# First tiles and weights of a conformer block over two DMA queues, normalized on VectorE and multiplied tile by tile, with the last chunk's halo columns copied one block ahead

## Chip, cores, metric

One core of one Trainium2 chip runs the whole program. The metric is the device time of one execution in microseconds (us); lower is better. Quoted times are medians of several runs with the lowest and highest in brackets; a trace is of one execution only.

## The reference

One conformer block with batch 2, 4000 tokens, width D = 512 and F = 2048, in bf16. `_layernorm` has no weights. Cut to what matters:

```python
h = _layernorm(x)                                  # x: [2, 4000, 512]
x1 = x + 0.5 * (_silu(h @ w_ff1_a) @ w_ff1_b)      # w_ff1_a: [512, 2048]
h = _layernorm(x1)                                 # one attention head of width 512
q, k, v = h @ w_q, h @ w_k, h @ w_v
x2 = x1 + (softmax(q k^T * D**-0.5) v) @ w_o
h = _layernorm(x2) @ w_pw1                         # w_pw1: [512, 1024]
h = h[..., :D] * sigmoid(h[..., D:])
dc = sum over i of hp[:, i:i+T] * dw[i]            # depthwise, width 3, hp padded by 1 on each side
dc = (dc - mean) / sqrt(var + 1e-5)                # mean, var per channel over all tokens
x3 = x2 + _silu(dc) @ w_pw2
x4 = x3 + 0.5 * (_silu(_layernorm(x3) @ w_ff2_a) @ w_ff2_b)
return _layernorm(x4)
```

Two places count here. At the start nothing can be multiplied before the first rows of `x` are loaded, normalized and transposed, and before the first columns of `w_ff1_a` have come. And the batch norm needs the statistics of all tokens, so that everything after the depthwise convolution of the last chunk waits for it.

## The kernel before

The tokens go in chunks of 508 (four tiles of 127 rows); the last chunk has 444. While the first rows come in, PE is kept busy with matmuls on zeros (`warm`), so that its clock is up when the real ones begin (in the traces a 508-column matmul takes 0.42 us at the slow clock of the start and 0.216 in the regular flow). Each tile's rows are loaded in two parts (112 and 15 rows). Engines are written as DVE (VectorE), ACT (ScalarE), POOL (GpSimd), PE (TensorE) and SP (the queue that issues most DMAs). Cuts are marked with `# ...`.

The loads. Six of the eight parts of the first four tiles are issued by SP, then all weights:

```python
    def load_rows(self, dst, src, writes, eng):
        k = self.S.dsems[self.nxt("ld", 16)]
        return self.S.dma(eng, k, *[lambda e, lo=lo, hi=hi: e.dma_start(dst[lo:hi], src[lo:hi])
                                     for lo, hi in self.ROWS], writes=writes)

    # ... in program():
        for ti in range(TPC):                       # TPC = 4
            self.load_rows(self.XT[ti], self.x_flat[ti * TILE:(ti + 1) * TILE, :], [self.bx[ti]], "ACT" if ti == 1 else "SP")
        for k in range(self.NWA):                   # NWA = 8 pieces of w_ff1_a, 256 columns each
            self.load_wa(i["w_ff1_a"], k, "SP")
            self.load_wb(i["w_ff1_b"], 2 * k, 2 * k + 2)
            # ...
```

The first layer norm: statistics on DVE, the power -1/2 on POOL (`ln_factor`), the normalization of three tiles on ACT and of the last on DVE. A block is one tile (or a pair of tiles) times the first four 128-column groups of `w_ff1_a`; groups 0 and 1 lie in weight piece 0, groups 2 and 3 in piece 1.

```python
    def ln_tiles(self, c, sl, prepare=None, engs=("ACT", "ACT", "ACT", "DVE"), src=None, lag=2):
        # ... finish(ti): sign product on DVE if the engine is ACT, then ln_norm on engs[ti]
        for ti in range(TPC):
            # ...
            self.ln_stats(c, sl, ti, src)
            # ...
            if ti >= lag:
                finish(ti - lag)
                yield ti - lag
            if lag == 1 or ti == TPC - 1:
                self.ln_mean(sl, ti)
                self.ln_factor(sl, ti)
        for ti in range(TPC - lag, TPC):
            finish(ti)
            yield ti

    def head(self):

        self.warm(14)
        self.rings["ln"] = 1
        self.early = [self.sbank() for _ in range(4)]

        def blocks(lo, hi):
            for f, (ps, b_ps) in enumerate(self.early):
                out = ps[:, lo * TILE:hi * TILE].rearrange("p (t k) -> p t k", t=hi - lo)
                for cc in range(DC):
                    self.mm(out, self.Wa[:, cc, f * 128:(f + 1) * 128], self.lnT[0][:, lo:hi, cc, 0:TILE],
                            cc == 0, cc == DC - 1, [self.b_Wa[f * self.NWA // FC]] + self.b_lnT[0][lo:hi], b_ps)

        for ti in self.ln_tiles(0, 0, lag=1):
            if ti:
                self.transpose_pe(ti - 1, 0, "ACT", (self.Yb[ti - 1], self.b_Y[ti - 1]))
            if ti == 2:
                blocks(0, 1)
        blocks(1, 2)
        self.transpose_pe(TPC - 1, 0, "DVE", (self.Yb[TPC - 1], self.b_Y[TPC - 1]))
        blocks(2, 4)
```

The last chunk's convolution. `conv_a` forms the gated values `G` of one 128-channel block; `halo_left` writes, on POOL, the one column left of them (copied from the chunk before) and the zero column right of the sequence's end. `finish` runs the depthwise convolution of the preceding block, its statistics, and with `conv_scale` a power on POOL of 0.55 us.

```python
    def conv_a(self, t, jj):
        # ...
        elif t == NCK - 1:
            self.halo_left(t, jj)
            self.S.op("DVE", lambda e: e.scalar_tensor_tensor(
                out=out, in0=ps[:, 0:W], scalar=2.0, in1=th, op0=ALU.mult, op1=ALU.mult),
                reads=[b_ps, self.b_th[k]], writes=wr)
        # ...

    # ... the loop over the four blocks of the last chunk:
        for jj in range(DC):
            self.conv_b(last, jj)
            # ...
            self.conv_a(last, jj)
            if jj > 1:
                self.conv_shift(jj - 2)
            if jj:
                finish(jj - 1)
            else:
                # ...
```

The gate names `Gl` and `Gr`, the columns that the halo writes, among what it writes (`wr`), so it stands behind `halo_left` wherever that comes in the program.

Of the kernel before, what the change touches and what calls it, by code (L numbers as in the profile page):

```python
# [15 lines left out]
TILE = 127  # L16
TPC = 4
# [10 lines left out]
DC = D // 128  # L28
FC = F // 128
# [51 lines left out]
class Sync:  # L81
# [103 lines left out]
        return None  # L185

    def dma(self, e, dkey, *fns, reads=(), writes=()):
        req = self._required(reads, writes)
        prev = self.count[dkey]
        if prev > 0:  # L190
            v = req.get(dkey)
            if v is None or v.val < prev:
                req[dkey] = Ev(dkey, prev, {})
        self._emit_waits(e, req)
        for fn in fns:
            fn(self.eng[e]).then_inc(self.sem[dkey], 16)
            self.count[dkey] += 16
        ev = Ev(dkey, self.count[dkey], dict(self.clock[e]))
        self._bind(ev, reads, writes)
        return ev  # L200

# [45 lines left out]
class Conformer:  # L247
# [315 lines left out]
        k = self.S.dsems[16 + self.nxt("tr", 12)]  # L563
        return self.S.dma("SP", k, lambda e: e.dma_start_transpose(dst, src), reads=reads, writes=writes)

    def load_rows(self, dst, src, writes, eng):
        k = self.S.dsems[self.nxt("ld", 16)]
        return self.S.dma(eng, k, *[lambda e, lo=lo, hi=hi: e.dma_start(dst[lo:hi], src[lo:hi])  # L568
                                     for lo, hi in self.ROWS], writes=writes)

    def store(self, dst, src, reads, writes):
        k = self.S.dsems[36 + self.nxt("st", 8)]
# [126 lines left out]

    def head(self):  # L700

        self.warm(14)
        self.rings["ln"] = 1
        self.early = [self.sbank() for _ in range(4)]

        def blocks(lo, hi):
            for f, (ps, b_ps) in enumerate(self.early):
                out = ps[:, lo * TILE:hi * TILE].rearrange("p (t k) -> p t k", t=hi - lo)
                for cc in range(DC):
                    self.mm(out, self.Wa[:, cc, f * 128:(f + 1) * 128], self.lnT[0][:, lo:hi, cc, 0:TILE],  # L710
                            cc == 0, cc == DC - 1, [self.b_Wa[f * self.NWA // FC]] + self.b_lnT[0][lo:hi], b_ps)

        for ti in self.ln_tiles(0, 0, lag=1):
            if ti:
                self.transpose_pe(ti - 1, 0, "ACT", (self.Yb[ti - 1], self.b_Y[ti - 1]))
            if ti == 2:
                blocks(0, 1)
        blocks(1, 2)
        self.transpose_pe(TPC - 1, 0, "DVE", (self.Yb[TPC - 1], self.b_Y[TPC - 1]))
        blocks(2, 4)  # L720

    def ln_mean(self, sl, ti):
        self.S.op("DVE", lambda e: e.bn_aggr(self.mv[sl][:, ti, :], self.st[sl][:, ti, :]),
# [355 lines left out]
    def conv_a(self, t, jj):  # L1079

        ps, b_ps = self.pw1(t, jj)
        k, gs, W = jj % 2, t % 2, width(t)
        th = self.th[k][:, 0:W]
        out = self.G[gs][:, jj, 1:1 + W]
        wr = [self.b_G[gs][jj], self.b_Gl[gs][jj], self.b_Gr[gs][jj]]
        if t == NCK - 2 and jj >= self.KEEP:

            asb, b_asb = self.asb[jj % 3], self.b_asb[jj % 3]
            self.act(asb, ps[:, 0:CHUNK], AF.Copy, [b_ps], [b_asb], scale=2.0)

            def gate(eng):
                self.S.op(eng, lambda e: e.tensor_tensor(out=out, in0=asb, in1=th, op=ALU.mult),
                          reads=[b_asb, self.b_th[k]], writes=wr)
                self.halo_left(t, jj)
                self.halo_right(t, jj)

            return gate
        elif t == NCK - 1:
            self.halo_left(t, jj)
            self.S.op("DVE", lambda e: e.scalar_tensor_tensor(  # L1100
                out=out, in0=ps[:, 0:W], scalar=2.0, in1=th, op0=ALU.mult, op1=ALU.mult),
                reads=[b_ps, self.b_th[k]], writes=wr)
        else:
            self.S.op("DVE", lambda e: e.scalar_tensor_tensor(  # L1104
                out=out, in0=th, scalar=1.0, in1=ps[:, 0:W], op0=ALU.add, op1=ALU.mult),
                reads=[b_ps, self.b_th[k]], writes=wr)
        if t < NCK - 1:
            self.halo_left(t, jj)
        self.halo_right(t, jj)
# [230 lines left out]
    def program(self, any_score):  # L1340
        i = self.i
# [4 lines left out]
        self.scr = self.OT.rearrange("p c k -> p (c k)")[:, 0:512]  # L1346

        for ti in range(TPC):
            self.load_rows(self.XT[ti], self.x_flat[ti * TILE:(ti + 1) * TILE, :], [self.bx[ti]], "ACT" if ti == 1 else "SP")
        for k in range(self.NWA):  # L1350
            self.load_wa(i["w_ff1_a"], k, "SP")
            self.load_wb(i["w_ff1_b"], 2 * k, 2 * k + 2)
            if k == 3:
                self.load_x(1)
# [71 lines left out]
        last = NCK - 1  # L1426
# [53 lines left out]
        def copy_away():  # L1480
            while copies:
                copies.pop(0)()

        for jj in range(DC):
            self.conv_b(last, jj)
            if jj == DC - 1:
                self.act(self.nr1, self.onef, AF.Silu, [self.b_onef], [self.b_nr1])
            copy_away()
            self.conv_a(last, jj)
            if jj > 1:  # L1490
                self.conv_shift(jj - 2)
            if jj:
                finish(jj - 1)
            else:
                f, copy = self.depthwise(tail - 1, DC - 1)
                f()
                copies.append(copy)
# [129 lines left out]
```

## Time and profile before

| | before |
|---|---|
| time, median of 4 runs | 2045.07 us (2044.95 to 2045.14) |
| span of the profiled execution | 2040.1 us |
| PE busy | 2029.2 us |
| start of PE's regular flow of 508-column matmuls | 13.06 us after the span's start |
| last swish of the first chunk (end of the batch norm's wait) | starts at 1543.50 us |

The page and the timelines that matter are shown in the prediction below, where they are read. One more view: the chain that ended last, followed back through the first 16 us. Columns are start, duration and what; "issue" is time in which an engine waited for nothing that the profile shows.

```profile
4.44 4.27 DMA wff<-in_w_ff_a_dram
...
8.75 0.62 PE s L506 x8
...
10.75 0.44 DVE work L553
...
11.33 2.77 PE s L506 x20
```

Before these lines the chain runs along SP's queue, which issues row after row and then weights; it goes into the second piece of `w_ff1_a` (issued at 4.44, landed 4.27 us later), and from there through PE and a copy on DVE to the flow. The start of the flow: the last row of the head mixes its last short matmuls with the first four long ones, and the row of four after it begins one group (0.87 us) after the flow did. The trace of this kernel is of an execution that took 2043.90 us, faster than each of the four timed ones.

### The profile page before, as it was taken

How to read it: one execution, taken by the hardware profiler on the slowest of the kernel's cores; microseconds unless marked ns; L12 is line 12 of the kernel's file. 1: busy time of each engine (PE TensorE's matmuls, PEld its weight loads, DVE VectorE, ACT ScalarE, POOL GpSimd, SP SyncE). 2: the span in 40 equal slices, each digit the busy share in tenths (PEclk: the TensorE clock that was granted, in tenths of full speed). 3: DMA queues.
4: the chain of work that ended last, by engine and by line, in shares of the span. 5: the costliest groups of instructions: out<-in, count | busy, mean ns of one | idle time of the engine just before them, and what ended most of it. 6: DMA issues, size and time to landing. Idle time of an engine off the chain costs nothing.

```text
span 2040.1 us, 24550 instructions
## 1 busy us (share of the span) xinstructions
PE 2029.2 (99%) x9665; PEld 1029.8 (50%) x9667; DVE 1081.1 (53%) x2187; ACT 746.9 (37%) x1280; POOL 107.7 (5%) x235
## 2 busy tenths in 40 slices
PE   9999999999999999999999999999999999999998
PEld 5555555554444444445444444444455555555555
DVE  4234443334556667666766676667674444434433
ACT  3433333333333333333333333333345443443433
POOL 1000000000000000000000000000011000000000
PEclk9999999999999999999999999999999999999999
DMA  8222245320101111114421111111143111111111
GB/s 185 52 62 62 53 100 126 96 70 8 27 16 26 25 33 26 25 25 95 108 57 23 26 28 33 24 26 26 44 135 93 32 31 42 32 31 42 28 35 38
DMA packets 253122, 104.43 MB, mean 51 GB/s; under 512 B 193412, under 2 KB 252487, under 8 KB 252999
## 3 DMA queue, kind: packets, MB, share of 16 engines
q1 hardware_dynamic: 252751, 102.61, 20.9%
q8 instruction: 78, 1.28, 0.3%
q14 instruction: 45, 0.37, 0.1%
q10 hardware_dynamic: 248, 0.18, 0.0%
HBM read 33.77 MB, written 23.34 MB: 28 GB/s over the span
## 4 chain that ended last, share of the span: by engine, by line
PE 98%; DVE 1%; ACT 0%; DMA 0%; SPq 0%; POOL 0%; issue 0%; DVEq 0%; ACTq 0%
PE s L506 56%; PE y L506 42%; ACT work L556 0%; DVE wff L1206 0%; DMA wff<-in_w_ff_a_dram 0%; SPq L568 0%; POOL work L1215 0%; DVE work L553 0%; DVE wff L1100 0%; PE y L534 0%; ACT keys L556 0%; DVE work L1213 0%; SPq L560 0%; DVE work L869 0%; DVE work L952 0%
## 5 line engine op out<-in xcount | busy, mean ns | idle before, releaser
L556 ACT ACTIVATE work<-s 128x508 bf16<-128x508 f32 (+3 forms) x1060 | 622.7, 588 | 1211.8 <-PE s L506 1208.2
L506 PE MATMUL s<-work,wff 128*128 128x508 bf16 (+5 forms) x2624 | 628.3, 371 | 1.5 <-DVE work L553 0.8
L506 PE MATMUL s<-work,keys 128*128 128x508 bf16 (+1 forms) x2048 | 516.7, 374 | 0.1
L506 PE MATMUL y<-work,keys 128*128 128x508 bf16 (+2 forms) x2048 | 504.2, 373 | 0.4 <-DVE work L553 0.4
L506 PE MATMUL y<-wff,work 128*127 128x512 bf16 (+1 forms) x2000 | 501.4, 378 | 0.0
L952 DVE TENSOR_TENSOR work<-work 128x508 f32<-128x508 f32 (+2 forms) x496 | 334.6, 675 | 282.9 <-ACT work L556 281.8
L506 PEld LDWEIGHTS s<-work,wff 128*128 128x128 bf16 x2624 | 252.3, 98 | 278.0 <-issue 5.0
L506 PEld LDWEIGHTS y<-wff,work 128*127 128x127 bf16 x2000 | 274.4, 137 | 170.8
L506 PEld LDWEIGHTS s<-work,keys 128*128 128x128 bf16 x2048 | 199.4, 98 | 231.9 <-issue 0.6
L506 PEld LDWEIGHTS y<-work,keys 128*128 128x128 bf16 (+1 forms) x2048 | 193.5, 97 | 234.0 <-issue 6.2
L755 DVE SCALAR_TENSOR_TENSOR xt<-y,xt 127x512 bf16<-127x512 f32 x125 | 77.8, 684 | 364.9 <-PE y L506 364.9
L618 DVE BATCH_NORM_STATS2 work<-xt 127x6 f32<-127x512 bf16 x311 | 195.5, 678 | 4.8 <-DMA xt<-in_x_dram 4.7
L506 PE MATMUL s<-work 128*127 128x512 bf16 (+3 forms) x776 | 196.2, 377 | 1.6 <-DVE work L1324 1.2
L625 POOL TENSOR_TENSOR work<-work 127x4 f32<-127x4 f32 (+1 forms) x76 | 76.5, 1007 | 1130.4 <-DVE work L623 1130.4
L506 PEld LDWEIGHTS s<-work 128*127 128x127 bf16 (+1 forms) x776 | 94.7, 124 | 75.7 <-issue 2.7
L638 DVE TENSOR_SCALAR work<-xt,work 127x512 bf16<-127x512 bf16 x306 | 110.4, 407 | 27.0 <-POOL work L625 23.2
L755 DVE SCALAR_TENSOR_TENSOR xt<-s,xt 127x512 bf16<-127x512 f32 x55 | 38.0, 692 | 148.6 <-PE s L506 148.6
L755 DVE SCALAR_TENSOR_TENSOR xt<-s,work,xt 127x512 bf16<-127x512 f32 x64 | 48.0, 750 | 30.8 <-PE s L506 30.2
L1104 DVE SCALAR_TENSOR_TENSOR wff<-wff,s 128x508 bf16<-128x508 f32 (+1 forms) x57 | 38.7, 679 | 41.4 <-PE s L506 41.2
L556 ACT ACTIVATE wff<-s 128x508 f32<-128x508 f32 (+1 forms) x67 | 39.5, 591 | 54.6 <-PE s L506 54.6
L556 ACT ACTIVATE work<-keys,work 128x508 bf16<-128x508 bf16 (+1 forms) x68 | 52.3, 775 | 0.8 <-DVE work L1220 0.7
L1185 POOL COPY wff<-wff 128x1 bf16<-128x1 bf16 x56 | 10.4, 187 | 637.8 <-DVE wff L1104 635.0
(92 smaller groups left out, 415.7 us busy)
## 6 DMA issues: line engine op xcount, KB each, us to landing
keys<-keysd SPq DMA_DIRECT2D x62, 128.0 KB, 2.3
keysd<-work SPq DMA_DIRECT2D x14, 448.0 KB, 3.2
out_dram<-work SPq DMA_DIRECT2D x14, 448.0 KB, 3.2
dcvd<-wff SPq DMA_DIRECT2D x48, 127.0 KB, 1.8
keys<-dcvd SPq DMA_DIRECT2D x12, 508.0 KB, 5.4
xt<-in_x_dram SPq DMA_DIRECT2D x13, 448.0 KB, 4.7
wff<-in_w_ff_a_dram SPq DMA_DIRECT2D x16, 256.0 KB, 5.0
work<-work SPq DMA_TRANSPOSE x208, 2.5
```

The lines of the kernel that those rows point to most:

```text
L506: self.S.op("PE", lambda e: e.matmul(out, lhsT, rhs, start=start, stop=stop, **kw), reads=reads, writes=[bank], inc=stop if inc is None el ...
L556: return self.S.op("ACT", lambda e: e.activation(out, in_, func, **kw), reads=reads, writes=writes)
L618: self.S.op("DVE", lambda e: e.bn_stats(self.st[sl][:, ti, 0:6], x), reads=[b_x], writes=[self.b_st[sl][ti]])
L625: S.op("POOL", lambda e: e.tensor_tensor(out=self.rs[sl][:, 0:n], in0=self.mv[sl][:, 0:n, 1], in1=self.neghalf[0:TILE, 0:n], op=ALU.pow), ...
L638: self.S.op("DVE", lambda e: e.tensor_scalar(out, x, self.mv[sl][:, ti, 0:1], self.rs[sl][:, ti:ti + 1], ALU.subtract, ALU.mult), reads=[b ...
L755: self.S.op("DVE", lambda e: e.scalar_tensor_tensor(out=self.XT[g][rows], in0=ps[rows], scalar=scalar, in1=self.XT[g][rows], op0=ALU.mult, ...
L952: S.op("DVE", lambda e, p=p, n=n, acc=acc: e.tensor_tensor(out=acc, in0=acc, in1=self.P[p][0:n, 0:W], op=ALU.add), reads=[self.b_P[p], sel ...
L1104: self.S.op("DVE", lambda e: e.scalar_tensor_tensor(out=out, in0=th, scalar=1.0, in1=ps[:, 0:W], op0=ALU.add, op1=ALU.mult), reads=[b_ps, ...
L1185: S.op("POOL", lambda e: e.tensor_copy(self.G[gs][:, jj, 0:1], self.G[gp][:, jj, CHUNK:CHUNK + 1]), reads=[self.b_G[gp][jj]], writes=[self ...
```

## The change

Its intent: bring PE's regular flow forward by issuing from SP and ACT at once, so that the weights don't stand behind six row loads; let DVE normalize each tile (0.41 us instead of ACT's 0.81) and PE multiply it as soon as it is there; and at the other end take the halo writes out from behind POOL's power, by writing them one block earlier. The diff, cut to its core:

```diff
@@ -185,17 +185,23 @@
         return None
 
     def dma(self, e, dkey, *fns, reads=(), writes=()):
+        return self.dma_by((e,) * len(fns), dkey, *fns, reads=reads, writes=writes)
+
+    def dma_by(self, engs, dkey, *fns, reads=(), writes=()):
+
         req = self._required(reads, writes)
         prev = self.count[dkey]
         if prev > 0:
             v = req.get(dkey)
             if v is None or v.val < prev:
                 req[dkey] = Ev(dkey, prev, {})
-        self._emit_waits(e, req)
-        for fn in fns:
+        for e in dict.fromkeys(engs):
+            self._emit_waits(e, req)
+        for e, fn in zip(engs, fns):
             fn(self.eng[e]).then_inc(self.sem[dkey], 16)
             self.count[dkey] += 16
-        ev = Ev(dkey, self.count[dkey], dict(self.clock[e]))
+        snap = dict(self.clock[engs[0]]) if len(set(engs)) == 1 else {}
+        ev = Ev(dkey, self.count[dkey], snap)
         self._bind(ev, reads, writes)
         return ev
 
@@ -563,10 +569,10 @@
         k = self.S.dsems[16 + self.nxt("tr", 12)]
         return self.S.dma("SP", k, lambda e: e.dma_start_transpose(dst, src), reads=reads, writes=writes)
 
-    def load_rows(self, dst, src, writes, eng):
+    def load_rows(self, dst, src, writes, engs):
         k = self.S.dsems[self.nxt("ld", 16)]
-        return self.S.dma(eng, k, *[lambda e, lo=lo, hi=hi: e.dma_start(dst[lo:hi], src[lo:hi])
-                                     for lo, hi in self.ROWS], writes=writes)
+        return self.S.dma_by(engs, k, *[lambda e, lo=lo, hi=hi: e.dma_start(dst[lo:hi], src[lo:hi])
+                                                for lo, hi in self.ROWS], writes=writes)
 
     def store(self, dst, src, reads, writes):
         k = self.S.dsems[36 + self.nxt("st", 8)]
@@ -699,25 +705,22 @@
 
     def head(self):
 
-        self.warm(14)
+        self.warm(13)
         self.rings["ln"] = 1
         self.early = [self.sbank() for _ in range(4)]
 
-        def blocks(lo, hi):
+        def blocks(ti):
             for f, (ps, b_ps) in enumerate(self.early):
-                out = ps[:, lo * TILE:hi * TILE].rearrange("p (t k) -> p t k", t=hi - lo)
                 for cc in range(DC):
-                    self.mm(out, self.Wa[:, cc, f * 128:(f + 1) * 128], self.lnT[0][:, lo:hi, cc, 0:TILE],
-                            cc == 0, cc == DC - 1, [self.b_Wa[f * self.NWA // FC]] + self.b_lnT[0][lo:hi], b_ps)
-
-        for ti in self.ln_tiles(0, 0, lag=1):
+                    self.mm(ps[:, ti * TILE:(ti + 1) * TILE], self.Wa[:, cc, f * 128:(f + 1) * 128],
+                            self.lnT[0][:, ti, cc, 0:TILE], cc == 0, cc == DC - 1,
+                            [self.b_Wa[f * self.NWA // FC], self.b_lnT[0][ti]], b_ps)
+
+        for ti in self.ln_tiles(0, 0, None, ("DVE",) * TPC, lag=1):
+            self.transpose_pe(ti, 0, "DVE" if ti == TPC - 1 else "ACT", (self.Yb[ti], self.b_Y[ti]))
             if ti:
-                self.transpose_pe(ti - 1, 0, "ACT", (self.Yb[ti - 1], self.b_Y[ti - 1]))
-            if ti == 2:
-                blocks(0, 1)
-        blocks(1, 2)
-        self.transpose_pe(TPC - 1, 0, "DVE", (self.Yb[TPC - 1], self.b_Y[TPC - 1]))
-        blocks(2, 4)
+                blocks(ti - 1)
+        blocks(TPC - 1)
 
     def ln_mean(self, sl, ti):
         self.S.op("DVE", lambda e: e.bn_aggr(self.mv[sl][:, ti, :], self.st[sl][:, ti, :]),
@@ -1096,7 +1099,6 @@
 
             return gate
         elif t == NCK - 1:
-            self.halo_left(t, jj)
             self.S.op("DVE", lambda e: e.scalar_tensor_tensor(
                 out=out, in0=ps[:, 0:W], scalar=2.0, in1=th, op0=ALU.mult, op1=ALU.mult),
                 reads=[b_ps, self.b_th[k]], writes=wr)
@@ -1346,9 +1348,13 @@
         self.scr = self.OT.rearrange("p c k -> p (c k)")[:, 0:512]
 
         for ti in range(TPC):
-            self.load_rows(self.XT[ti], self.x_flat[ti * TILE:(ti + 1) * TILE, :], [self.bx[ti]], "ACT" if ti == 1 else "SP")
+            self.load_rows(self.XT[ti], self.x_flat[ti * TILE:(ti + 1) * TILE, :], [self.bx[ti]],
+                           ("SP", "ACT" if ti < 2 else "SP"))
+        for k in range(2):
+            self.load_wa(i["w_ff1_a"], k, "ACT")
         for k in range(self.NWA):
-            self.load_wa(i["w_ff1_a"], k, "SP")
+            if k > 1:
+                self.load_wa(i["w_ff1_a"], k, "SP")
             self.load_wb(i["w_ff1_b"], 2 * k, 2 * k + 2)
             if k == 3:
                 self.load_x(1)
@@ -1481,6 +1487,7 @@
             while copies:
                 copies.pop(0)()
 
+        self.halo_left(last, 0)
         for jj in range(DC):
             self.conv_b(last, jj)
             if jj == DC - 1:
@@ -1489,9 +1496,12 @@
             self.conv_a(last, jj)
             if jj > 1:
                 self.conv_shift(jj - 2)
+            if 0 < jj < DC - 1:
+                self.halo_left(last, jj + 1)
             if jj:
                 finish(jj - 1)
             else:
+                self.halo_left(last, 1)
                 f, copy = self.depthwise(tail - 1, DC - 1)
                 f()
                 copies.append(copy)
```

## The prediction

> **What bounds the kernel now.** I read the page first: the busy shares, then the chain that ended last. The chain's two PE lines already hold 98% of the span, and PE is busy 2029.2 of 2040.1 us, so the whole kernel has 10.9 us in which PE does nothing, and no change that leaves PE's own work alone can win more than a part of that.
>
> ```profile
> span 2040.1 us, 24550 instructions
> PE 2029.2 (99%) x9665; PEld 1029.8 (50%) x9667; DVE 1081.1 (53%) x2187; ACT 746.9 (37%) x1280; POOL 107.7 (5%) x235
> PE s L506 56%; PE y L506 42%; ACT work L556 0%; DVE wff L1206 0%; DMA wff<-in_w_ff_a_dram 0%; SPq L568 0%; POOL work L1215 0%; DVE work L553 0%; DVE wff L1100 0%; PE y L534 0%; ACT keys L556 0%; DVE work L1213 0%; SPq L560 0%; DVE work L869 0%; DVE work L952 0%
> ```
>
> The change touches two short stages only. The first is the head, before PE runs without gaps. The timeline of PE alone shows it: columns are start, duration, what, and in brackets the idle time before it and what ended it.
>
> ```profile
> 1.17 4.59 PE L506 MATMUL s<-work 128*128 128x508 bf16 x14 [1.17 <-DVE work L1324]
> 6.27 0.40 PE L521 MATMUL y<-work 127*128 127x127 bf16 x4 [0.51 <-ACT work L556]
> 7.21 0.40 PE L521 MATMUL y<-work 127*128 127x127 bf16 x4 [0.54 <-ACT work L556]
> 7.78 0.61 PE L506 MATMUL s<-work,wff 128*128 128x127 bf16 x8 [0.17 <-ACT work L556]
> 8.75 0.62 PE L506 MATMUL s<-work,wff 128*128 128x127 bf16 x8 [0.36 <-DMA wff<-in_w_ff_a_dram]
> 10.33 0.39 PE L521 MATMUL y<-work 127*128 127x127 bf16 x4
> 11.33 2.77 PE L506 MATMUL s<-work,wff 128*128 128x254 bf16 x20 [0.61 <-DVE work L553]
> ```
>
> The bracketed idles after the warm matmuls sum to 2.19 us: the normalized tiles come late from ACT, the second weight piece comes late by DMA (8.75), and the last pair of tiles waits for a copy out of PSUM (11.33). The x20 row is 16 matmuls of 254 columns and then the first 4 of 508; from there on PE has no gap. With 16 at 0.1077 us that regular flow begins at 11.33 + 1.72 = 13.05. This time is what the head has to bring forward.
>
> The second stage is the last chunk's convolution, between 1530 and 1545 us. There PE has few gaps of its own; the chain goes through DVE, POOL and ACT. Here are rows of the timeline of all engines:
>
> ```profile
> 1534.19 0.22 DVE L1213 BATCH_NORM_AGGREGATE work<-wff 128x2 f32<-128x15 f32 x1
> 1534.49 0.55 POOL L1215 TENSOR_TENSOR work<-work 128x1 f32<-128x1 f32 x1 [1.38 <-DVE work L1213]
> 1535.11 0.10 POOL L1188 MEMSET wff<- 128x1 bf16 x1
> 1535.34 0.62 DVE L1100 SCALAR_TENSOR_TENSOR wff<-s,wff 128x444 bf16<-128x444 f32 x1 [0.93 <-POOL wff L1188]
> 1538.51 0.62 DVE L1100 SCALAR_TENSOR_TENSOR wff<-s,wff 128x444 bf16<-128x444 f32 x1 [0.93 <-POOL wff L1188]
> 1542.00 0.82 ACT L556 ACTIVATE work<-keys,work 128x508 bf16<-128x508 bf16 x1
> 1543.50 0.81 ACT L556 ACTIVATE work<-keys,work 128x508 bf16<-128x508 bf16 x1 [0.68 <-DVE work L1220]
> ```
>
> The gate (L1100) of blocks 2 and 3 waits 0.93 us each for two one-column halo writes on POOL. They sit on POOL behind the 0.55 us power of the preceding block (L1215), which itself waits for that block's statistics. The lag ends in ACT's last swish of the first chunk, which starts 0.68 us after ACT was free.
>
> **What the Trainium skill says.** (1) "DMA: Bandwidth & Descriptors", section "Issuing engines are not separate DMA queues": starting transfers from several engines saves only the sequencer's issuing time; they share the same 16 DMA engines. The trace agrees on the size: the six row loads hold SP's queue 2.67 us, about 0.45 each, and the first weight piece goes out at 3.44. (2) The same page, "Queues, rings and completion order": each DMA engine goes round-robin between queues, so early weight pieces on ACT's queue do not stand behind SP's rows, but take turns with them. No view here shows that yet. (3) "TensorE: Matmul & The Clock Gate", "Wait — 56ns, not 53.3ns?": a warm matmul costs N/2.4 GHz + 2.5 ns. The trace agrees: 16 blocks of 127 columns hold 0.90 us in the chain, 0.056 each. Four sets of 127 therefore cost almost what two sets of 254 do. (4) "ScalarE: Activation LUTs", "What ACT_TABLE_LOAD costs": 1283 ns for a load, and 186 + 0.833 N ns for an ACTIVATE plus 93 ns for each pointer operand, so 0.80 us at N = 512 with scale and bias. The trace has 1.28 and 0.808.
>
> **Head, step by step.** Removed: three ACT norms of 0.81 and three DVE sign products (L676, 0.16). Added: three DVE norms, 0.41 each by the one that DVE has now (L638). Replaced: 16 matmuls of 254 by 32 of 127 (1.72 against 1.80 us), and one warm matmul less. Moved: one part of each of the first two tiles and the first two weight pieces go out on ACT's queue.
>
> Start. Tile 0's small part goes out at 1.18 on SP now and lands about 2.1 us later, and the statistics start at 3.47. On ACT's queue it goes out at 0.73, with 2.4 to land (ACT's own figure): 3.13. DVE's memsets end at 3.21, so T0 = 3.25.
>
> DVE per tile, with the delays of the present trace (aggregate 0.73 after statistics begin, POOL's power 0.28 later, DVE's use of it 0.65 to 0.67 after that begins, next aggregate 0.36 after a norm begins, next statistics 0.11 later): the norms end at T0 + 2.09, + 3.40, + 4.71, + 6.02, that is 5.34, 6.65, 7.96, 9.27. A tile now takes 1.31 where the statistics loop took 1.00, because power and norm lie in series on DVE's order. The last norm ends later than today's 8.56; the first ends earlier than ACT's 6.21.
>
> PE: transposes at 5.40, 6.71, 8.02, 9.33 (4 x 0.056 each). A copy on ACT opens the block 1.14 after its transpose began (0.42 to the copy, 0.58 in it, 0.14 to PE), the one on DVE 1.00. Block 0 follows transpose 1: 6.95 to 7.85. Block 1: 8.25 to 9.15. Transpose 3 then block 2: 9.56 to 10.46. Block 3's copy is ready at 10.33, so it runs 10.46 to 11.36, with no wait. Then matmul group 4 needs the PSUM bank of group 0, whose Silu starts 0.43 after block 3 began (0.23 for four matmuls, 0.2 latency) and lasts 0.59: 11.48, PE at 11.6. The regular flow starts at 11.6 instead of 13.05: **1.45 us** less.
>
> Weights: the two first pieces go out about 1.75 and 2.2 on ACT. The first piece today takes 2.8 us to land; with contention I allow 3.5 to 4.2, so 5.3 and 6.4, before their use at 6.95 and 7.4. Today the second goes out at 4.44 and takes 4.27. Rows 2 and 3 keep their places on SP (2.07 and 2.96 for their last parts, about 2.0 to land); sharing adds perhaps 0.5, so 4.6 and 5.5, against their use at 5.40 and 6.71.
>
> **Tail, step by step.** No work is added: four copies and four memsets on POOL stand earlier in its order. POOL's order of after.py shows just that: two powers now come after the next halo pair. Gate 2 then waits for PE alone, whose eight matmuls end at 1534.85: 1534.95 instead of 1535.34. Gate 3: PE ends 1537.55, so 1537.65 instead of 1538.51. PE is not faster for it, as its groups abut from 1530.48 to 1538.60. The depthwise of block 3 also needs a PSUM bank that ACT frees at 1539.36 behind its table load, as today. DVE: its statistics of block 2 end by 1539.6, aggregate 1539.85; block 3's first statistics 1540.1, the second after PE's 1540.76: 1540.86 to 1541.56; aggregate to 1541.84; POOL to 1542.47; shift to 1542.7. ACT is free at about 1542.75. So the swish starts near 1542.77: **0.73 us** less, and what follows (copies, four swishes, norms, all ACT in a row) moves with it.
>
> Sum: 1.45 + 0.73 = 2.2 us, 2045.0 - 2.2 = **2042.8 us**; span of the profile about 2037.9.
>
> **Rivals.** *DMA takes the gain back:* weights beside rows 2 and 3 delay the statistics, or piece two lands after 7.4. For: the same 16 engines, and 256 KB a piece. Against: those engines moved only 118 GB/s between 4 and 5 us, and the slack is 0.8 to 1.2 us. It would leave 0.5 to 1 us of the head: 2043.3 to 2043.8. *The norm chain becomes the bound for good:* DVE's 1.31 a tile against ACT beside DVE. For: the last norm really comes 0.7 later. If a tile took 1.6, the head would win only 0.6: 2043.7. *The tail wait is replaced:* ACT was due behind its table load, or the aggregate of block 3 ends when it did. For: PE's block 3 depthwise does not move. Then the tail gives 0.2 and the total is 2043.3. *The end hides it:* the regular flow waits later for weights. Against: from 13 us to the first chunk's end PE waits for nothing.
>
> **Range and chances.** Both parts as worked out give 2042.8; a bit luckier (earlier rows, no bank wait) 2042.2; one part half lost 2043.5, both half lost 2043.9. Runs agree within 0.2 us. So 2042.1 to 2043.9. Two per cent is 41 us, four times all of PE's idle time: faster 0.005, same 0.99, slower 0.005.
>
> **What would show it.** Head right: first transposes at 5.4, no PE wait on a weight DMA, norms about 1.3 apart, PE's 127-column blocks ending near 11.4 and a short wait on ACT before the 508-column matmuls at 11.6. Tail right: no wait of L1100 on POOL L1188, gates directly behind PE, the swish without its 0.68 idle. Wrong: statistics that wait for rows 2 or 3, a weight wait in block 0, or a swish still waiting for L1220 by more than 0.3.

## The result, and the profile after

The changed kernel takes 2042.55 us (2041.63 to 2043.21, four runs) against 2045.07 (2044.95 to 2045.14, four runs) before. The ratio is 0.9987, 95% interval 0.9970 to 1.0005. By the class of 2% the two are the same, and the interval includes 1; the gain is 2.5 us of medians, and the question is where it comes from and whether it is all the change's. The trace after is of the fastest of its four executions (2041.63 us).

The page after, the lines that answer to those in the prediction:

```profile
span 2037.6 us, 24579 instructions
PE 2028.8 (100%) x9682; PEld 1030.0 (51%) x9682; DVE 1081.6 (53%) x2187; ACT 743.6 (36%) x1277; POOL 107.6 (5%) x235
```

PE's busy time is the same within 0.4 us; its idle time has gone from 10.9 to 8.8 us. ACT has lost its three norms. The timeline of PE alone in the head (start, duration, what, and in brackets the idle time before and what ended it):

```profile
1.18 4.43 PE L512 MATMUL s<-work 128*128 128x508 bf16 x13 [1.18 <-DVE work L1326]
5.45 0.39 PE L527 MATMUL y<-work 127*128 127x127 bf16 x4
6.65 0.40 PE L527 MATMUL y<-work 127*128 127x127 bf16 x4 [0.81 <-DVE work L644]
6.88 1.06 PE L512 MATMUL s<-work,wff 128*128 128x127 bf16 x16
8.17 0.40 PE L527 MATMUL y<-work 127*128 127x127 bf16 x4 [0.23 <-DVE work L644]
...
9.66 3.08 PE L512 MATMUL s<-work,wff 128*128 128x127 bf16 x36
12.58 1.03 PE L512 MATMUL y<-wff,work 128*127 128x512 bf16 x4
```

No row waits for a weight any more, and the transposes come with the norms (L644). The flow begins at 12.58 - 0.87 = 11.71 instead of 13.06. The chain that ended last now begins elsewhere, in the same window as the chain shown for the kernel before:

```profile
3.02 4.07 DMA xt<-in_x_dram
...
7.11 0.27 DVE work L624
...
7.72 0.41 DVE work L644
...
9.82 1.79 PE s L512 x32
```

What bounds the head is no longer a weight but the last 15 rows of the fourth tile: issued at 3.02, landed 4.07 us later, where in the kernel before such a part landed in about 2.0. DVE's statistics (L624) waited 0.42 us for it, in the timeline of all engines:

```profile
7.11 0.69 DVE L624 BATCH_NORM_STATS2 work<-xt 127x6 f32<-127x512 bf16 x1 [0.42 <-DMA xt<-in_x_dram]
```

In DVE's order the third tile's norm (7.72) stands behind these statistics, and so waits with them. The list of DMA issues of the first 3.6 us shows both sides (KB each, median us from issue to landing). Before:

```profile
wff<-in_w_ff_a_dram SPq DMA_DIRECT2D x1, 256.0 KB, 2.8
xt<-in_x_dram SPq DMA_DIRECT2D x3, 15.0 KB, 2.0
```

After:

```profile
wff<-in_w_ff_a_dram ACTq DMA_DIRECT2D x2, 256.0 KB, 4.2
xt<-in_x_dram SPq DMA_DIRECT2D x2, 15.0 KB, 3.7
```

So the rows became slower once the two weight pieces were issued beside them; that the pieces are the cause is tested in e9. In the tail, from the timeline of all engines:

```profile
1533.41 0.55 POOL L1217 TENSOR_TENSOR work<-work 128x1 f32<-128x1 f32 x1 [1.23 <-DVE work L1215]
...
1533.87 0.62 DVE L1102 SCALAR_TENSOR_TENSOR wff<-s,wff 128x444 bf16<-128x444 f32 x1 [0.54 <-PE s L512]
...
1540.92 1.59 ACT L562 ACTIVATE work<-keys,work 128x508 bf16<-128x508 bf16 x2
```

The gate (now L1102) waits for PE alone, and ACT's two swishes run back to back (x2 in one row), where the second had 0.68 us of idle before it. The view of waits of this stretch says the same in two lines. Before (waiter, what it waited for: us in total, times, longest):

```profile
DVE wff L1100 <- POOL wff L1188: 1.9, 2, 0.9
ACT work L556 <- DVE work L1220: 0.7, 1, 0.7
```

After, neither is there; the gate's line is

```profile
DVE wff L1102 <- PE s L512: 1.2, 3, 0.5
```

To account for the spans I cut each trace at the same events: the start of the flow, a middle that ends before the last chunk's convolution, a tail part from there to beyond it (about 1490 to 1552 us in the kernel before), and the time from the issue of the last store to the end of the span. The four columns don't add up to the span, as stretches between them are left out; these agree within 0.02 us.

| trace | flow starts | middle | tail part | last store to end | span |
|---|---|---|---|---|---|
| before | 13.06 | 1451.86 | 61.35 | 3.35 | 2040.06 |
| after | 11.71 | 1452.14 | 60.63 | 2.67 | 2037.58 |
| difference | -1.35 | +0.28 | -0.72 | -0.68 | -2.48 |

The head gave 1.35 us and the tail 0.72. The other two lie where the change touches nothing: 0.28 us is one pause of PE in mid-kernel (at about 961 us), and the last store landed sooner in this execution. The store was issued at 2036.71 before and at 2034.90 after: from issue to issue the difference is 1.81 us, where the span differs by 2.48. In the traces of all kernels below this landing takes from 2.67 to 4.06 us without any order by kernel. A difference of one microsecond between two single executions can therefore be the store's alone, and the experiments are read by their timed rounds together with the cut-up traces.

### The profile page after: what moved, and what is told of

It is laid out like the page before. It is cut to its first block, busy times and chain, and to the rows that moved or that the text cites. A ratio compares the mean times of both kernels' runs of the same rounds, so it can differ in the third digit from the quotient of the medians.

```text
span 2037.6 us, 24579 instructions
## 1 busy us (share of the span) xinstructions
PE 2028.8 (100%) x9682; PEld 1030.0 (51%) x9682; DVE 1081.6 (53%) x2187; ACT 743.6 (36%) x1277; POOL 107.6 (5%) x235
## 3 DMA queue, kind: packets, MB, share of 16 engines
q8 instruction: 78, 1.28, 0.3%
## 4 chain that ended last, share of the span: by engine, by line
PE 98%; ACT 1%; DVE 0%; DMA 0%; SPq 0%; issue 0%; ACTq 0%
PE s L512 56%; PE y L512 42%; ACT work L562 0%; DMA xt<-in_x_dram 0%; ACT keys L562 0%; SPq L574 0%; PE y L540 0%; DVE work L559 0%; ACT L562 0%; PE y L527 0%; DVE work L872 0%; DVE work L955 0%; DVE wff L1208 0%; DVE wff L1095 0%; ACT wff L562 0%
## 5 line engine op out<-in xcount | busy, mean ns | idle before, releaser
L512 PE MATMUL s<-work,wff 128*128 128x508 bf16 (+4 forms) x2640 | 628.3, 369 | 0.6 <-DVE work L559 0.2
L624 DVE BATCH_NORM_STATS2 work<-xt 127x6 f32<-127x512 bf16 x311 | 195.3, 676 | 4.9 <-DMA xt<-in_x_dram 4.8
L512 PE MATMUL s<-work 128*127 128x512 bf16 (+4 forms) x775 | 195.8, 377 | 1.2 <-DVE work L1326 1.2
L512 PEld LDWEIGHTS s<-work 128*127 128x127 bf16 (+2 forms) x775 | 94.7, 124 | 74.9 <-issue 2.7
L644 DVE TENSOR_SCALAR work<-xt,work 127x512 bf16<-127x512 bf16 x309 | 111.5, 406 | 27.2 <-POOL work L631 23.2
```

The costliest lines, as they stand in the source:

```text
L512: self.S.op("PE", lambda e: e.matmul(out, lhsT, rhs, start=start, stop=stop, **kw), reads=reads, writes=[bank], inc=stop if inc is None el ...
L624: self.S.op("DVE", lambda e: e.bn_stats(self.st[sl][:, ti, 0:6], x), reads=[b_x], writes=[self.b_st[sl][ti]])
L644: self.S.op("DVE", lambda e: e.tensor_scalar(out, x, self.mv[sl][:, ti, 0:1], self.rs[sl][:, ti:ti + 1], ALU.subtract, ALU.mult), reads=[b ...
```

## The experiments

Theory: the head gains about 1.4 us because weights and norms both come earlier, the tail 0.7 us because the gate no longer stands behind POOL's power, and the two add. Rivals: one part of the head does all (the queues alone, or the norms alone); the rows' delay beside the weights takes back part of the head; part of the gain is the spread of the runs. All kernels gave the reference's result. "Gain" below is the difference of mean times against the kernel before in the same rounds, timed; "flow" is its start in the trace (13.06 before).

| run | timed, median (lowest to highest) | gain | flow | tail part | store |
|---|---|---|---|---|---|
| e1 after again | 2042.77 (2041.95 to 2043.24) | 1.63 | 12.15 | 60.62 | 3.96 |
| e2 head only | 2042.97 (2042.83 to 2043.20) | 1.27 | 12.03 | 61.35 | 2.95 |
| e3 tail only | 2042.95 (2042.71 to 2043.77) | 1.08 | 13.05 | 60.67 | 2.95 |
| e4 DVE norms only | 2043.68 (2043.26 to 2044.03) | 0.63 | 12.88 | 61.37 | 3.39 |
| e5 queues only | 2044.10 (2043.20 to 2044.31) | 0.38 | 12.76 | 61.35 | 3.95 |
| e6 ten warm matmuls | 2042.61 (2042.15 to 2043.75) | 1.56 | 12.03 | 60.63 | 4.06 |
| e7 one piece beside the rows | 2042.97 (2042.58 to 2043.16) | 1.44 | 12.04 | 60.64 | 3.68 |
| e8 e6 and e7 together | 2042.78 (2041.23 to 2043.33) | 1.80 | 11.87 | 60.63 | 3.95 |
| e9 weights behind the rows | 2050.10 (2049.10 to 2051.43) | -5.29 | 19.50 | 60.64 | 3.26 |
| e10 after, a third time | 2042.78 (2042.21 to 2043.66) | 1.92 | 12.17 | 60.64 | 3.67 |
| e11 four pieces beside the rows | 2042.76 (one run) | | 12.14 | 60.63 | 3.71 |
| e12 as e9, mended | 2043.95 (2042.55 to 2046.57) | 0.68 | 11.53 | 60.65 | 3.82 |

The kernel before, in the same rounds: 2044.22 (2043.82 to 2044.78) beside e1 to e4, 2044.36 (2043.88 to 2045.02) beside e5 to e8, 2044.92 (2043.99 to 2045.37) beside e9 to e11, 2044.41 (2043.98 to 2045.32) beside e12. Five runs of each kernel (one of e11), nine of the one before. e1 to e4 and e9 to e11 ran on one chip, e5 to e8 and e12 on another.

How far the times carry: the 95% interval of every ratio of these experiments is about 0.0014 to either side, some 2.8 us, and includes 1 for all but e9 (1.0012 to 1.0040), so by this interval no gain is clear. What can be said is that all runs of the changed kernel, and of e2, e3, e6, e7 and e8, lie below all runs of the kernel before in the same rounds (e3's by 0.05 us only); those of e4, e5 and e12 overlap with them. The finer readings rest on the traces, one for each kernel.

### e1: the changed kernel again

No edit. It tells what of the first result repeats.

> The changed kernel as it is, to see its spread. Prediction theory: regular flow begins 1.35 us earlier than before (trace offset at 39 us), tail offset 0.73 more at 1550 us; median 2042.5 to 2043.2. The four runs so far spread over 1.6 us where before spreads over 0.2. Theory A (spread comes from when the first tiles and weights land in the head): the profile of another run shows a different wait of the statistics on the last row tile (0.42 in the first profile) or of block 0 on a weight. Theory B (hiccups anywhere in PE's instruction stream and the last store): the head is the same within 0.1 us and the difference sits elsewhere.

Measured: gain 1.63 us, ratio 0.9992. The tail repeats to 0.01 us, the head doesn't: the flow starts at 12.15, 0.44 later than in the first trace. The last store took 1.28 us longer, so both theories hold in part. PE's timeline shows why:

```profile
1.18 5.68 PE L512 MATMUL s<-work 128*128 128x508 bf16 x13 [1.18 <-DVE work L1326]
6.65 0.67 PE L527 MATMUL y<-work 127*128 127x127 bf16 x8
7.87 1.05 PE L512 MATMUL s<-work,wff 128*128 128x127 bf16 x16 [0.55 <-ACT work L562]
```

Columns are as before. The same 13 warm matmuls took 5.68 us here and 4.43 in the first trace. All of them ran at the slow clock (0.42 us apart); in the first trace the full clock was granted 4.2 us after the span's start, here at about 6.7, by the trace's record of the clock. The first tile was normalized by 5.33, but its transpose stands behind the warm matmuls and ran at 6.65, together with the second tile's (x8). Block 0 then waited for the copy of that transpose, and from 7.87 on PE had no gap in which to catch up. So the head's gain depends on when the full clock is granted, and in the 14 traces this first comes between 3.86 and 7.21 us. The warm-up that used to be free is now on the path: in e3, with the head of before, the full clock came at 7.21, the warm matmuls ended at 7.29, and the flow still began at 13.05.

The rows were late in e1 too (landed 7.24, the statistics waited 0.57). In the four traces in which the rows bind (the first, e2, e6, e10) the flow begins 4.62 us after the fourth tile's rows have landed, every time. By this e1's rows alone would have allowed 11.86, so that about 0.3 of the 0.44 us is the warm-up's, as an estimate.

### e2: the head alone, e3: the tail alone

e2 is the changed kernel with the halo as before; e3 is the kernel before with the halo of the change.

```diff
 # e2, against the changed kernel             # e3, against the kernel before: the reverse
+            self.halo_left(t, jj)             # in conv_a, last chunk
-        self.halo_left(last, 0)
-            if 0 < jj < DC - 1:
-                self.halo_left(last, jj + 1)
-                self.halo_left(last, 1)
```

> Head part alone, halo order as before. Prediction theory: about 1.35 us below before, 2043.7, and no change in the tail (gates of blocks 2 and 3 wait 0.93 on POOL again). If the spread comes from the head (theory A) these runs spread over 1 us or more; if it comes from the tail or anywhere, as in e3.

> Halo part alone, head as before. Prediction theory: 0.73 us below before, 2044.3, by the swish that starts without its 0.68 us of idle; runs within 0.3 us of each other as with before. Rival (the wait is replaced by one on ACT or on the last aggregate): 0.2 us or less, 2044.9.

Measured: e2 gains 1.27 timed (ratio 0.9994), and its flow starts 1.03 earlier with the tail at 61.35, as before. e3 gains 1.08 timed (0.9995), its flow starts at 13.05 and its tail part is 0.68 shorter. The timed gains add to 2.35, more than e1's 1.63. Both parts' traces had a short landing of the last store (2.95, e1 3.96), but each is one of five executions, so that this doesn't explain the means, and the difference stays open. In the traces without the store, 1.03 + 0.68 = 1.71 stands against e1's 0.91 + 0.73 = 1.64: each part shows with or without the other, and they add within the head's own scatter. The expectation that the runs' spread comes from the head failed: e2's five lie within 0.37 us, e3's within 1.06. In e2's tail the swish still waits for the last shift, in the timeline of all engines:

```profile
1542.47 0.81 ACT L562 ACTIVATE work<-keys,work 128x508 bf16<-128x508 bf16 x1 [0.68 <-DVE work L1223]
```

In e3's it doesn't:

```profile
1542.02 1.59 ACT L556 ACTIVATE work<-keys,work 128x508 bf16<-128x508 bf16 x2
```

The tail's mechanism is shown: moving the four halo writes on POOL (a copy and a memset each) and nothing else takes the wait away.

### e4: norms on DVE and blocks by tile, with the loads of before; e5: the loads alone

Both without the halo part.

```diff
 # e4, against e2
-                           ("SP", "ACT" if ti < 2 else "SP"))
-        for k in range(2):
-            self.load_wa(i["w_ff1_a"], k, "ACT")
+                           ("ACT",) * 2 if ti == 1 else ("SP",) * 2)
         for k in range(self.NWA):
-            if k > 1:
-                self.load_wa(i["w_ff1_a"], k, "SP")
+            self.load_wa(i["w_ff1_a"], k, "SP")

 # e5, against e2: head() as before
-        self.warm(13)
+        self.warm(14)
-        for ti in self.ln_tiles(0, 0, None, ("DVE",) * TPC, lag=1):
+        for ti in self.ln_tiles(0, 0, lag=1):
 # ... and blocks(lo, hi), transposes and pairs as before
```

> Only the norms on VectorE and the blocks by tile; all loads on the queues and in the order of before, halo as before. Worked out like the prediction: second weight piece still lands at 8.7, so half of block 0 waits for it; transpose 3 at about 10.3, regular flow at about 12.6: 0.45 us below before, 2044.6. Rival (the norm chain alone makes the gain, the weights are hidden): the full 1.35, 2043.7.

> Only the loads moved (two row parts and two weight pieces on ACT's queue); norms on ACT, pairs of blocks, 14 warm matmuls and halo order as before. Worked out like the prediction: statistics start 0.22 earlier, no wait of block 0 on the second weight piece, transpose 3 at about 9.7, copy at 10.1, pair block at 10.65, regular flow near 12.4, 0.7 us before the 13.06 of before. With e4 (flow 12.88) the parts would add to 0.85 of the 0.9 to 1.35 that the whole head gave. Rival (the norms on VectorE are needed for any gain): flow at 12.9 or later.

Measured: e4 gains 0.63 timed, 0.18 in the flow (12.88); e5 0.38 timed, 0.30 in the flow (12.76). Both fall short of what I expected. In e4 PE comes to block 0 earlier and then stands before the same late piece of weights, which landed at 8.99 in this trace. I had counted with 8.7, and the 0.28 us between make up the whole difference to the 12.6 expected:

```profile
9.03 0.62 PE L512 MATMUL s<-work,wff 128*128 128x127 bf16 x8 [1.19 <-DMA wff<-in_w_ff_a_dram]
```

In e5 the weights are there (6.76 by the record of landings, used after 8), but the 14 warm matmuls took 5.84 us and ended late, as in e1, and the last pair of tiles (at 11.03) still waits 0.61 us for a copy on DVE, as in the kernel before.

What follows: each half of the head leaves the other half's wait standing. By their flows 0.18 + 0.30 = 0.48 us alone, together 0.89 to 1.35. That is how two waits behave that run side by side and end near each other: taking one away uncovers the other. e5's late clock and e4's late piece make each part look too small, so the split between the two is not exact. That neither gave the whole gain is seen in these two traces; the timed runs (0.63 and 0.38) point the same way but overlap with those of before.

### e6: ten warm matmuls; e7: one piece of weights beside the rows; e8: both

e1 put the warm-up on the path, and the first trace the fourth tile's rows. e6 takes the one away, e7 is to relieve the other.

```diff
 # e6, against the changed kernel
-        self.warm(13)
+        self.warm(10)
 # e7, against the changed kernel: the second piece on SP, right behind the rows
-            self.load_wa(i["w_ff1_a"], k, "ACT")
+            self.load_wa(i["w_ff1_a"], k, ("ACT", "SP")[k])
```

> The changed kernel with 10 warm matmuls instead of 13. The profile e1 showed all 13 at the slow clock (0.42 each, to 6.65 us), so that the first transpose, ready at 5.4, waited for them and the flow began at 12.15 instead of 11.72. Theory: with 10 they end by 5.4 even at the slow clock, so flow at 11.7 to 12.0 whatever the clock did. Rival: fewer warm matmuls keep the clock slow for longer, and block 0 runs at half speed (1.8 us instead of 0.9): flow at 12.2 or later.

> The changed kernel with only the first weight piece on ACT's queue; the second goes out on SP right after the rows. In three profiles of the changed head the statistics of the last row tile waited 0.42, 0.57 and 0.73 us for the rows. Theory (weights beside the rows on the same engines delay them): the wait falls under 0.3 and the flow starts 0.2 to 0.4 earlier when the clock is warm, about 11.45. Rival (rows arrive when they do, whatever the weights): same wait of 0.4 to 0.7, flow as before, or later because the second piece lands after 7.4.

> Both of e6 and e7. If both theories hold this is the best: flow 11.4 to 11.6 in any clock phase, time 0.2 to 0.5 us below the changed kernel. If either rival holds, no better than the changed kernel.

Measured: gains 1.56, 1.44 and 1.80 against 1.63 and 1.92 for the changed kernel itself; none is better clear of the spread. The traces say why. In e6 the first transpose runs when its tile is ready, also with little warming:

```profile
5.39 0.40 PE L527 MATMUL y<-work 127*128 127x127 bf16 x4
```

and block 0 ran at full speed (1.06 us for 16). But its chain is then the rows', with the flow at 12.03:

```profile
3.01 4.39 DMA xt<-in_x_dram
```

In e7 it was the other way round: its rows landed at 7.40 (0.70 us of wait), no earlier than with two pieces ahead of them, and its chain begins with the warm matmuls and has no DMA in it:

```profile
1.17 5.41 PE s L512 x13
```

PE's weight load also stood 0.17 us before the second piece, which landed at 8.14. In e8 the rows did come earlier (6.66, no wait of the statistics), but the second piece, sent later, landed at 7.98, and block 0 waited for it:

```profile
8.02 0.62 PE L512 MATMUL s<-work,wff 128*128 128x127 bf16 x8 [0.53 <-DMA wff<-in_w_ff_a_dram]
```

So three things end close to one another: warm-up, rows, second piece. Taking one away shows the next.

### e9: both pieces behind the rows

To see what the rows do without weights beside them. The first piece goes out on SP after the rows, the second on ACT after its table load; ten warm matmuls.

```diff
 # e9, against the changed kernel with ten warm matmuls
-        for k in range(2):
-            self.load_wa(i["w_ff1_a"], k, "ACT")
-            if k > 1:
+            if k != 1:
                 self.load_wa(i["w_ff1_a"], k, "SP")
+        self.load_wa(i["w_ff1_a"], 1, "ACT")     # behind constants() and the table load
```

> The changed kernel with 10 warm matmuls, and the first two weight pieces behind the rows: the first on SP after the last row part, the second on ACT after its table load. The record of landings says that the last row part landed at 4.84 to 4.94 in the three traces with the old order and at 6.66 to 7.41 in the seven with weights beside the rows. Theory (weights beside the rows delay them): the last rows land near 4.9 again, the statistics wait for nothing, norms at 4.92, 6.18, 7.44, 8.70; the pieces land near 6.3 and 7.0; flow at 11.45 to 11.6 against 11.72 to 12.15 of the changed kernel, time 0.3 to 0.5 us below it. Rival (the rows were late for another cause, such as two queues on one row tile): last rows land after 6.5 still, flow at 12.0.

Measured: 5.29 us slower (ratio 1.0026, interval 1.0012 to 1.0040), by a fault of my edit. The second piece was emitted behind the other loads, got the semaphore of the first one in the round of 16, and had therefore to wait until that one had landed. It went out at 6.58 and landed at 13.96. Meanwhile PE lost its full clock, too: by the record of the clock it had it from 3.86 to 7.27 us and again from 17.51 on. In PE's timeline block 0 waits for the piece:

```profile
14.01 1.03 PE L512 MATMUL s<-work,wff 128*128 128x127 bf16 x8 [5.13 <-DMA wff<-in_w_ff_a_dram]
```

The time says nothing for the theory, but the rows' part of the trace does. With no weights beside them the last row parts landed at 4.24 and 4.92, where the changed kernel has 5.45 and 7.09 (5.45 and 7.55 in e10, on the same chip in the same rounds). From the issues of the first 3.6 us, and the fourth tile's statistics:

```profile
xt<-in_x_dram SPq DMA_DIRECT2D x2, 15.0 KB, 2.0
...
6.61 0.65 DVE L624 BATCH_NORM_STATS2 work<-xt 127x6 f32<-127x512 bf16 x1
```

They waited for no DMA. The norms of this run start at 4.92, 6.18, 7.43 and 8.69, that is 1.26 apart without any wait for a DMA. The rows' issues are the same in both kernels to 0.02 us; what differs before the rows are in is the two weight pieces on ACT from 1.80 on. (ACT's table load also comes earlier, at 1.80 instead of 2.81, but so it does in e12, where one piece goes out at 1.88 and the rows are late.) The 2.2 us in the fourth tile's landing are the pieces' doing. All traces agree: without a piece ahead of them these rows landed at 4.84 to 4.94 in four, with one or more at 6.19 to 7.55 in ten.

This run also shows the next bound. In the rows' four traces the flow begins 3.99 us after the third tile's norm; here that norm starts at 7.43, so that with no wait for rows, weights or warm-up the flow would begin at about 11.42 (an estimate). Another order of the loads alone could then gain at most some 0.3 us over the first trace's 11.71.

### e10: the changed kernel a third time; e11: four pieces beside the rows; e12: e9, mended

e11 doubles the suspected cause. e12 lets the constants and the table load come first in the program, so that the loads keep their own semaphores.

```diff
 # e11, against the changed kernel
-        for k in range(2):
+        for k in range(4):
             self.load_wa(i["w_ff1_a"], k, "ACT")
-            if k > 1:
+            if k > 3:
 # e12, against the changed kernel with ten warm matmuls
+        self.constants()                        # both moved up from below; a guard is cut here
+        self.act(self.nr1, self.onef, AF.Silu, [self.b_onef], [self.b_nr1])     # the table load
         for k in range(2):
-            self.load_wa(i["w_ff1_a"], k, "ACT")
+            self.load_wa(i["w_ff1_a"], k, ("SP", "ACT")[k])
```

> The changed kernel again, beside e9 on the same chip. Theory: last rows land at 6.9 to 7.4 and the statistics wait 0.4 to 0.8 for them; flow between 11.7 and 12.2 by the phase of the clock; tail 60.63 as in the other traces with the halo part; last store 2.6 to 4.1 us from its issue to the end.

> The suspected cost doubled: four weight pieces on ACT's queue beside the rows instead of two. Theory: the rows are no earlier than with two (7.0 to 7.4) or later, the ACT table load moves from 2.8 to about 3.8, the first second-layer pieces on SP come later or equal; flow at 12.0 or later. If the rows do not get later than 7.4, the delay comes from the first pieces alone, as the later ones are issued after the rows.

> As e9, but the second weight piece is put into the program ahead of the other pieces, so that it no longer shares a semaphore with the first one (in e9 it waited for that, went out at 6.6 behind nine other pieces and landed at 13.96). Theory (weights beside the rows delay them; both behind the rows lets the rows land near 4.9): statistics without waits, norms at 4.92, 6.18, 7.43, 8.69 as e9 had them; pieces land near 6.4 and 7.2, ACT's piece taking turns with SP's; flow at 11.45 to 11.7, time 2042.2 to 2042.6, 0.3 to 0.5 us below the changed kernel in the mean. Rival (the engines are short of bandwidth, and what the rows win the weights lose): second piece after 7.5, wait in block 0, flow at 11.9 or later, no gain.

Measured, e10: gain 1.92, flow 12.17; this time the rows are the bound, with the longest wait seen:

```profile
7.57 0.70 DVE L624 BATCH_NORM_STATS2 work<-xt 127x6 f32<-127x512 bf16 x1 [0.88 <-DMA xt<-in_x_dram]
```

e11: the fourth tile's rows landed at 7.20, within the 6.19 to 7.55 of one or two pieces. Doubling made nothing worse; the flow (12.14) was set by the warm matmuls, which took 5.68 us as in e1. The third and fourth piece are issued on ACT only at about 2.8 and 3.4 us, when the rows are out or nearly so (the last part at 3.0). In the kernel before, too, a piece was issued right behind the rows, at 3.44, and they landed at 4.86 all the same. So what delays them is what goes out ahead of their last parts. One piece of 256 KB is enough for a delay: with one at 1.80 to 1.88 they landed at 6.19, 6.66 and 7.40 (e12, e8, e7), with two or more at 6.96 to 7.55. Whether the second one adds to it is not settled by so few traces.

e12: the second piece did not come behind the table load; it was issued on ACT at 1.88, beside the rows, so that this is rather e8 with the pieces exchanged. Its one trace is the best head of all. The fourth tile's rows landed at 6.19 and the statistics never waited; block 0 waited 0.18 us for the first piece, and the flow began at 11.53:

```profile
7.23 1.07 PE L512 MATMUL s<-work,wff 128*128 128x127 bf16 x16 [0.18 <-DMA wff<-in_w_ff_a_dram]
```

But its timed runs are not: 2042.55, 2042.65, 2044.00, 2043.95 and 2046.57, in the mean 0.68 better than before and so worse than the changed kernel. The slowest of them lists a clock of 0.998. Ten warm matmuls may leave the clock slow for longer in some executions, or the first piece of weights, now behind the rows, may come late in some; those executions left no trace, so this stays open. For the slowest a lost clock is likely: e9, whose trace shows one, lists 0.997 and 0.998, and all other executions here 0.999 or 1.000. No version here beats the changed kernel clear of the spread.

## Why the prediction was right, and where it was not

It gave 2042.8 us with 2042.1 to 2043.9; the medians measured were 2042.55, 2042.77 and 2042.78 in three sessions. Point by point:

- **PE bounds the kernel, and only the edges can gain.** Right: PE's busy time moved by 0.4 us, its idle time by 2.1.
- **Tail, 0.73 us.** Right in size and mechanism: 0.72, 0.73, 0.71 in the three traces of the changed kernel, 0.68 with the tail alone. The gates wait for PE, and the swish for nothing. In the first trace the two gates begin at 1533.87 and 1536.58 and the swish at 1541.70; by the 1.07 us that the first trace is ahead there (1.35 less the pause of 0.28), these are the prediction's 1534.95, 1537.65 and 1542.77 to 0.01.
- **Head, 1.45 us.** Too large as a mean: 1.35, 0.91 and 0.89, in the mean 1.05. Two terms of the working failed.
  - *Rows 2 and 3 landing at 4.6 and 5.5* ("sharing adds perhaps 0.5"): they landed at 5.02 to 5.59 and 6.19 to 7.55 in all kernels with weights beside the rows ahead of them, at 4.24 and 4.92 without (e9). In the changed kernel (7.09, 7.24, 7.55) the slack that I counted took most of it up, and 0.42, 0.57 and 0.88 us of wait were left. This is the rival "DMA takes the gain back", in part true; I had dismissed it by the 118 GB/s between 4 and 5 us, but that was how idle the engines were without the early weights; with them the same stretch has 299 GB/s.
  - *Transposes at 5.40*: I took it that the warm matmuls would end before. In the first trace they did (5.45). In e1 they ended 1.2 us later, as the clock was granted later. That wait (about 0.3 us of the flow, as estimated under e1) is in none of the prediction's steps; I removed one warm matmul in the count without asking how long 13 last at the slow clock.
- **Norms 1.31 apart, ending at 5.34 to 9.27.** Nearly: 1.26 apart where nothing waits (e9), first end 5.33; DVE's chain as such bounded the head in none of the traces, and would do so at about 11.42.
- **Weights at 5.3 and 6.4, before their use.** Landed at 5.67 and 6.87 in the first trace; a little late, but before block 0 needed them (6.88 for the first; half of the block later, about 7.3, for the second). No wait, as said. That the two queues take turns agrees with the record of landings: the first piece's run from 4.56 to 5.67, among those of the third tile's rows (to 5.45), and the second's from 5.51 to 6.87, among those of the fourth tile's (to 7.09).
- **The two parts add.** Right in the traces, within the head's scatter: 1.71 from the parts, 1.64 together, without the store.

That the first result came within 0.3 us of the prediction was partly luck. The head's mean of 1.05 and the tail's 0.72 add to 1.77 us, not to the 2.2 worked out. The first session's kernel before was also slower (2045.07) than in the later rounds (2044.22 to 2044.92), which has nothing to do with the change. Nor do the two spans confirm the 2.5 us: besides 1.35 and 0.72 their difference holds 0.68 from a quick last store and -0.28 from a pause in mid-kernel. The timed gains of 1.63 and 1.92 us in the later rounds are the better measure of the change.

## What to carry to other kernels

When a start-up has several waits that end near one another, work out the landing of everything once more under the changed order: an early transfer takes its time from what is in flight beside it, here about 2 us from the fourth tile's rows, and the slack of those is part of the price. Warm-up work on PE is only free while nothing real stands behind it; count it at the slow clock. And when a gain is a thousandth, cut the trace at fixed events and compare pieces, since the last store alone varied by 1.39 us, nearly as much as the change was worth.

## What the Trainium skill lacked or had wrong

- "DMA: Bandwidth & Descriptors", section "Issuing engines are not separate DMA queues", says that issuing from several engines saves only the sequencer's time. The runs agree that no bandwidth is won (some 1.04 MB of rows and weights had landed by about 7 us before and after). But as the weights are issued sooner, it also changes what lands first: the first weight piece landed at 5.67 instead of 6.28 and the second at 6.87 instead of 8.71, and the fourth tile's last rows at 7.09 instead of 4.86. The page gives no size for such a delay.
- "TensorE: Matmul & The Clock Gate", section "What's actually happening", tells of a free-running window of 3413 ns and advises not to fit a model to a specific count of cold matmuls, as the ramp is under 1% of a typical span. No run shows the window itself, but the start of the full clock varies as it says (3.86 to 7.21 us): the same 13 matmuls took 4.43 us in one execution and 5.68 in another. What it lacks is the case of a head: these 1.2 us put the first transpose on the path and cost about 0.3 us (estimated under e1) of the 1.2 that the head would have gained there.
- No page gives the spread of a kernel's last store from issue to the end of the span: 2.67 to 4.06 us over 14 traces.
